# Two input blocks held in SBUF between two sweeps, together with a new table of rank shifts

## The chip, the cores and the metric

The kernel runs on one core of one Trainium2 chip, as one launch. The metric is device microseconds (us) of that core. Most executions agree within 0.3%. The times are about 1.7 us longer than the span of the trace in the same execution.

Five engines matter here: TensorE (PE in the profile, PEld for its weight loads), VectorE (DVE), ScalarE (ACT), GpSimd (POOL) and SyncE (SP). SyncE computes nothing; all loads and stores of any size go through its DMA queue (SPq in the timelines), in the order in which they are issued.

## The reference, cut to what matters

Four residual blocks in a row, linear attention (A), gated unit (B), A again, B again, with shared weights; the outputs are the result and the gradients of x and of all weights. The sequence has 2048 rows of 512, in bfloat16.

```python
x = A_x
x = x + _A_ref(_layernorm(x, axis=-1), A_wqkv, A_wo)
x = x + _B_ref(_layernorm(x, axis=-1), B_w_gate, B_w_up, B_w_down)
x = x + _A_ref(_layernorm(x, axis=-1), A_wqkv, A_wo)
x = x + _B_ref(_layernorm(x, axis=-1), B_w_gate, B_w_up, B_w_down)
...
_out, _vjp = jax.vjp(_f, A_x, A_wqkv, A_wo, B_w_gate, B_w_up, B_w_down)
_grads = _vjp(grad_out)
```

The first A needs its input twice: once for the keys and values of all rows (sweep 1), and again, after the sum over all rows is known, for the residual addition (sweep 2). Between the two lies a barrier.

## The kernel before: the parts that matter

The kernel is a list of pieces. A piece is a short run of instructions with its dependencies, its cost on TensorE and the cost of what follows on other engines. A planner written in Python runs once, while the program is built. It gives each piece a rank (the length of the longest path from it to the end), and plays the pieces through a model of the engines; whenever an engine of the model is free, it gets the ready piece of the highest rank. The order that comes out is fixed into each engine's list of instructions. The table OFFSETS is added to the ranks: a positive shift lets a piece go earlier, a negative one later.

```python
for u in self.pieces:
    u.prio += self.offsets.get(u.key.rpartition(".")[0] if u.key.count(".") > 1 else u.key, 0.0)
```

Sweep 1 loads the eight input blocks (256 rows each) and gives each buffer back after its layer norm. Sweep 2 loads them again, last block first:

```python
def sweep1(k):
    ...
    for b in range(NBLK):
        G.load(f"LX.{b}", lambda b=b: ld(b), BLK, [f"LN0.{b - 3}.1"], "+t2")
        if b == 0:
            G.load("WK", lambda: load_w4(k, wq_[:, D:2 * D], "wk"), 2 * BLK, ["LX.0"], "+w4")
        layernorm(k, 0, b, lambda b=b: xin[b], [[f"LX.{b}", f"LN0.{b - 1}.1@s", f"<GS0.{b - 3}.3"]] * 2)
        G.free("-t2", [f"LN0.{b}.{j}@h" for j in range(2)])
        ...

def sweep2(k):
    ...
    def xin(b):
        t = t2(k, "x0l", [P, 2, D])
        nc.sync.dma_start(out=t[:], in_=tok3(k.x_in, last - b))
        return t
```

The last stage, from about 720 us on, computes the weight gradients: groups of 32 matmuls each. One operand of a group comes from HBM, turned over by a transposing DMA (the tile `dw_set`); a group ends with an evacuation into a small buffer `dw_o` of a ring, and a store:

```python
def load_set(src, r0, n, deps=()):
    nm = f"S{ns[0]}"
    ...
    nc.sync.dma_start_transpose(out=t[:, :, 0:n], in_=src[r0:r0 + n, :])
...
G.store(f"SJ{gi}", lambda: nc.sync.dma_start(out=out_ap, in_=st["o"][0:r, 0:n]), r * n * 2 / 1e6, [f"J{gi}.3"], "-s1")
```

The sets are S0, S1, ...; the groups' matmuls are J0, J1, ... and their stores SJ0, SJ1, ... in the table's language.

Of the kernel before, what the change touches and what calls it, by code (L numbers as in the profile page):

```python
# [25 lines left out]
NBLK = S // TB  # L26
# [48 lines left out]
class Plan:  # L75
# [210 lines left out]
ACCJ, ACCY = 11, 7  # L286
KEEP = (3, 3)
KEEPX, KEEPQ = 3, 2
SBT = {2: range(8), 0: range(0), 1: range(0)}
SUMS = {1: ([0, 1], -1), 3: ([2, 3], 1), 5: ([4, 5], 3), 6: ([6], 5), 7: ([7], 6)}  # L290
MSUMS = {1: ([0, 1], -1), 3: ([2, 3], 1), 5: ([4, 5], 3), 7: ([6, 7], 5)}
PB1 = (0.0, 0.0)
OFFSETS = """
    DE0:3=-81,7=+11 DE2:1=+97 DH2:1=+84 DK0:4=+21 DK2:4=-48 DP0:1=-15,2=+49,3=+71
    DP2:0=-18,2=+21,3=+4,4=+10,5=+30,6=-198 DT0:+67 DW1:1=-50,3=-1 DW3:0=+95,1=+64,4=-2,7=+13 Fg3:11=+28 Fh1:12=-14
    Fh3:4=-25 G1:0=-49,1=-15 G11:7=+97 G3:4=+64,5=+66,7=+38 GS0:2=+20,5=+17,6=-68 GS2:6=+30 K0:0=-18 K2:2=+31
    LB3:4=-3,7=+65 LDH2:6=+11,7=+11 LDL0:5=+36 LDL2:1=-69,2=-7,7=+23 LDP2:6=+2 LDQ2:6=-3 LDX0:4=-5 LG3:0=+58,1=+39
    LN0:2=-53,4=-92,7=-170 LP0:2=-11,3=-11 LQ2:2=-2,3=-15,5=+7 LS1:1=-7 LX:7=+127 LX0:4=+76,5=+35 MS0:5=-306
    MS2:1=-65,3=-1 Q0:1=-63,4=-40,5=-57,7=+64 Q2:2=+18 RX2:2=+69 S1:-43 S30:-17 SG2:-21 SH3:7=-73 SK2:7=-70 SM2:-73
    SN0:2=-193,5=-178,6=-178 SN2:0=-118 SO3:7=-56 SPK2:3=+30 SQ0:1=+127,2=+8 SQ2:7=-122 SU1:5=+8 SV1:1=-89  # L300
    SV3:0=+40,7=-139 TB1:5=-12 TG0:1=+2,2=+6,4=-176,5=-76,6=+6 TG2:4=+100,6=+71 TK0:0=+111,4=+293,5=+613,7=+151
    U0:1=-40 WP2:3=+87 WT2:3=-45 Y1:4=-9 Y33:0=-16,1=-13 YA2:5=+8,6=-1 ZE0:2=+19
    ZE2:0=+69,1=+72,2=+89,3=+160,4=+184,5=+142,6=+105 ZS0:3=+16,5=+30 ZS2:7=+28
"""
BLK = S * D * 2 / 8e6
TOKENS = dict(mm=5, acc=2, tp=1, t2=BUFS["t2"], xb=BUFS["xb"], s1=BUFS["s1"], w4=BUFS["w4"], w11=BUFS["w11"],
# [83 lines left out]
def t2(k, name, shape=None, dt=BF16):  # L390
    return k.p1.tile(shape or [P, NDC, TB], dt, name=name, tag="t2", bufs=BUFS["t2"])
# [420 lines left out]
def a_p2(k, l, b, xin_fn, deps):  # L812

    nc, G = k.nc, k.G
    A = k.A[l]
    st = {}
    n = f"{l}.{b}"
    C = NBLK - 1 - b
    B = b if l else C

    def lx():
        st["xin"] = xin_fn()

    def den():
        pq = A.pq[b]
        ps = tpps(k, [P, 2, H], "den_ps", F32)
        for j in range(2):
            for c in range(NDC):
                nc.tensor.matmul(ps[:, j, :], lhsT=pq[:, c, tslice(j)], rhs=A.Z[:, c, :],
                                 start=(c == 0), stop=(c == NDC - 1))  # L830
        yield
        dn = k.p1.tile([P, 2, H], F32, name="dn", tag="dn", bufs=2)
        nc.vector.tensor_scalar(dn[:], ps[:], EPS, None, ALU.add)
        yield
        r = k.p1.tile([P, 2, H], F32, name="rcp", tag="rcp", bufs=2)
        nc.vector.reciprocal(r[:], dn[:])
        for j in range(2):
            yield
            st["rx", j] = s1(k, "rx")
            src = r[:, j, :].unsqueeze(2).to_broadcast([P, H, D // H])  # L840
            dst = st["rx", j][:].rearrange("p (h e) -> p h e", h=H)
            if l == 0:
                nc.scalar.copy(dst, src)
            else:
                nc.gpsimd.tensor_copy(dst, src)

    def turn(j):
        if j == 0:
            st["rT"] = t2(k, "rTx", [P, 2, NDC, P])
        nc.sync.dma_start_transpose(out=st["rT"][:, j, :, :], in_=st["rx", j][:])  # L850

    def spread(hf):
        if hf == 0:
            A.pn[b] = t2(k, "pnT")
            A.rphi[b] = t2(k, "rphiT")
        sl = slice(2 * hf, 2 * hf + 2)

        def by_tile(t):
            return t[:, sl, :].rearrange("p c (j t) -> p c j t", j=2)
        rT = st["rT"][:, :, sl, :].rearrange("p j c t -> p c j t")  # L860
        nc.vector.tensor_tensor(by_tile(A.pn[b]), by_tile(A.pq[b]), rT, ALU.mult)
        yield
        rphi = by_tile(A.rphi[b])
        nc.vector.tensor_scalar(rphi, by_tile(A.pq[b]), -EPS, 1.0, ALU.add, ALU.min)
        yield
        nc.vector.tensor_tensor(rphi, rphi, rT, ALU.mult)

    def y(j):
        if j == 0:
            k.x[l, b] = xb(k, "xa") if l == 0 else st["xin"]  # L870
        ps = mmps(k, [P, D], "ya_ps")
        for c in range(NDC):
            nc.tensor.matmul(ps[:], lhsT=A.pn[b][:, c, tslice(j)], rhs=A.Wp[:, c, :], start=(c == 0), stop=(c == NDC - 1))  # L873
        yield
        nc.vector.scalar_tensor_tensor(k.x[l, b][:, j, :], ps[:], 1.0, st["xin"][:, j, :], ALU.mult, ALU.add,
                                       accum_out=k.sx[l + 1][:, 2 * b + j:2 * b + j + 1])
    if l and b < KEEPX:
        G.add("LX" + n, lx, 0.0, [f"LN2.{C}.{j}" for j in range(2)])
    else:
        G.load("LX" + n, lx, BLK if l == 0 else 2 * BLK, [f"YA{l}.{b - 2}.1"] + ([f"SX1.{C}"] if l else []) + deps, "+t2" if l == 0 else "+xb")  # L880
    eng = "P" if l else "A"
    G.add("DE" + n, den, 8 * 0.027, [f"Q{n}.0", f"Q{n}.1", f"ZZ{l}", f"<YA{l}.{b - 2}.1"],
          [("V", 0.22, "+dn -tp"), ("V", 0.55, "-dn"), (eng, 0.65, "+s1 @0"), (eng, 0.65, "+s1")], "+tp")
    for j in range(2):
        G.load(f"RX{n}.{j}", lambda j=j: turn(j), BLK, [f"DE{n}" + ("" if j else "@0")] + ([f"~RX{n}.0"] if j else []), "-s1" if j else "+t2 -s1", turn=True)
    for hf in range(2):
        G.add(f"SP{n}.{hf}", lambda hf=hf: spread(hf), 0.0, [f"RX{n}.{j}" for j in range(2)] + ([f"~SP{n}.0"] if hf else []),
              [("V", 0.42, "@pn"), ("V", 0.29), ("V", 0.42)], "" if hf else "+t2 +t2")
    G.free("-t2", [f"SP{n}.{hf}" for hf in range(2)])
    pn = [f"SP{n}.{hf}@pn" for hf in range(2)]  # L890
    G.free("-t2", [f"SP{n}.0", f"SP{n}.1"])
    G.store(f"SN{n}", lambda: nc.sync.dma_start(out=dmaj(k.pnT_d[l], B), in_=A.pn[b][:]), BLK, pn)
    G.store(f"SR{n}", lambda: nc.sync.dma_start(out=k.rphi_d[l][B * P:(B + 1) * P, :], in_=flat(A.rphi[b][:])), BLK, [f"SP{n}.{hf}" for hf in range(2)], "-t2")
    G.free("-t2", [f"SN{n}", f"<YA{n}.1"])
    if l == 0:
        G.free("-t2", [f"YA{n}.{j}" for j in range(2)])
    for j in range(2):
        G.add(f"YA{n}.{j}", lambda j=j: y(j), 4 * C512, pn + ["LX" + n] + [f"WP{l}.{c}" for c in range(NDC)] + ([f"<YA{n}.0"] if j else []),
              [("V", 0.69, "-mm")], "+mm +xb" if j == 0 and l == 0 else "+mm")
# [4 lines left out]
def a_b1(k, l, b, deps):  # L904
# [58 lines left out]
    for j in range(2):  # L963
        G.add(f"CA{n}.{j}", lambda j=j: cast(j), 0.0, [f"LB{lx}.{b}.{j}", "LN_" + n, f"<MS{l}.{b - 2 if b % 2 else b - 3}.3"]
              + ([f"CA{n}.0"] if j else []), [("A", 0.62)], "" if j else "+t2")
    if b in SBT[l]:
        def turn(j):
# [461 lines left out]
def glu_bwd(k, l, b):  # L1429
# [28 lines left out]
    def chunk(p):  # L1458
        w = pw(p)
        cs = slice(2 * p, 2 * p + len(pair_chunks(p)))  # L1460
        dps = (proj_tiles if b in SBT[l] else proj)(k, k.wdT, st["gT"], p, "dhh_ps")
        yield
# [89 lines left out]
def sweep1(k):  # L1552
    nc, G = k.nc, k.G
    k.x, k.dx, k.hT = {}, {}, {}
    xin = {}
    last = NBLK - 1

    def ld(b):
        xin[b] = t2(k, "x0", [P, 2, D])
        nc.sync.dma_start(out=xin[b][:], in_=tok3(k.x_in, b))  # L1560
    wq_ = k.w["wqkv"]
    for b in range(NBLK):
        G.load(f"LX.{b}", lambda b=b: ld(b), BLK, [f"LN0.{b - 3}.1"], "+t2")
        if b == 0:
            G.load("WK", lambda: load_w4(k, wq_[:, D:2 * D], "wk"), 2 * BLK, ["LX.0"], "+w4")
        layernorm(k, 0, b, lambda b=b: xin[b], [[f"LX.{b}", f"LN0.{b - 1}.1@s", f"<GS0.{b - 3}.3"]] * 2)
        G.free("-t2", [f"LN0.{b}.{j}@h" for j in range(2)])
        a_k(k, 0, b, True, b >= TURN0)
        a_q(k, 0, b, True, [] if b < 2 else [f"<K0.{last}.1"])
    G.load("WQ", lambda: load_w4(k, wq_[:, 0:D], "wq"), 2 * BLK, ["LX.2", "WK"], "+w4")  # L1570
    G.load("WV", lambda: load_w4(k, wq_[:, 2 * D:3 * D], "wv"), 2 * BLK, ["LX.4", "WQ"], "+w4")
    G.load("WO", lambda: load_w4(k, k.w["wo"], "wo"), 2 * BLK, ["LX.5", "WV"], "+w4")
    G.free("-w4", ["<K2.%d.1" % last])
    G.free("-w4", [f"<Q2.{last}.1"])
    G.free("-w4", ["<KV2"])
    G.free("-w4", ["<WP2.3"])
    a_barrier(k, 0)


def sweep2(k):  # L1580
    nc, G = k.nc, k.G
    last = NBLK - 1

    def xin(b):
        t = t2(k, "x0l", [P, 2, D])
        nc.sync.dma_start(out=t[:], in_=tok3(k.x_in, last - b))
        return t
# [316 lines left out]
```

## Time and profile before

| | before |
|---|---|
| time, median of the first 3 runs | 1088.78 us (1088.7 to 1089.19) |
| span of the profiled execution | 1084.6 us, mean granted clock 0.998 |
| TensorE busy | 1055.2 us |
| DMA volume | 240.33 MB |
| largest waits of TensorE | 7.0 us start, 2.1 us barrier, 1.8 us first transposed set |

The second row hides something that matters later: 0.998 is not full clock. A stretch of 3.4 us at half clock in a span of 1085 us lowers the mean by 3.4 / 2 / 1085 = 0.0016. So 0.998 is about one such stretch, 0.997 two, 0.995 three, and 1.000 none. The record of the clock begins at about 12 us; the matmuls before it are slow in every kernel (four key matmuls take 1.86 us at 8.79 us and 1.03 us at 221.87 us, before) and are not counted in these means.

### The profile page before, as it was taken

What the parts mean: (1) busy time and instruction counts of PE and PEld (TensorE: products, weight loads), DVE (VectorE), ACT (ScalarE), POOL (GpSimd) and SP (SyncE); (2) the same over time, 40 slices, a digit from 0 to 9 for tenths busy, and PEclk for the clock granted to TensorE, in tenths of its full rate; (3) what the DMA queues carried; (4) which work ended last, traced back from release to release, by engine and by line L of the source; (5) the groups of instructions that cost most, each with busy time, mean ns of one, the idle gap of its engine ahead of it and who ended that gap; (6) DMA issues with size and microseconds to landing.
All of it is one profiled execution on the core that took longest, in us unless ns stands there. A gap on an engine that the chain in (4) does not pass through costs nothing.

```text
span 1084.6 us, 19597 instructions
## 1 busy us (share of the span) xinstructions
PE 1055.2 (97%) x7265; PEld 692.1 (64%) x7360; DVE 637.3 (59%) x1558; ACT 358.0 (33%) x717; POOL 186.7 (17%) x457
## 2 busy tenths in 40 slices
PE   6989999999999999999899999999999999999998
PEld 3667667666566667675566666656554466666787
DVE  6897787689866887788766658768754000000010
ACT  6765565455243333332244433431211000000010
POOL 3145676526012120200000000000000000000000
PEclk9999999999999999999999999999999999999999
DMA  7868898987998777866998799779999999999970
GB/s 237 261 178 277 227 269 246 241 228 194 239 230 210 189 203 192 210 166 162 247 246 257 212 279 285 212 168 237 224 275 267 264 225 216 236 225 227 209 173 20
DMA packets 508208, 240.33 MB, mean 222 GB/s; under 512 B 333808, under 2 KB 493264, under 8 KB 506064
## 3 DMA queue, kind: packets, MB, share of 16 engines
q1 hardware_dynamic: 508112, 239.07, 87.6%
q8 instruction: 57, 0.93, 0.4%
q14 instruction: 39, 0.32, 0.1%
HBM read 61.93 MB, written 95.72 MB: 145 GB/s over the span
## 4 chain that ended last, share of the span: by engine, by line
PE 83%; DVE 5%; DMA 3%; issue 1%; POOL 1%; SPq 1%; ACT 1%; DVEq 0%; ACTq 0%; POOLq 0%
PE dw_ps L1786 25%; PE dha_ps L1155 7%; PE g_ps L1214 6%; PE dh_acc L1296 6%; PE u_ps L1214 6%; PE dhh_ps L1214 6%; PE dh_acc L1294 6%; PE y_acc L1266 3%; PE y_ps L1416 3%; PE dpk_ps L1139 3%; PE m_ps L998 2%; PE ya_ps L873 2%; PE dpn_ps L937 2%; PE k_ps L599 1%; PE g_ps L625 1%
## 5 line engine op out<-in xcount | busy, mean ns | idle before, releaser
L1786 PE MATMUL dw_ps<-dw_set,h 128*128 128x352 bf16 (+2 forms) x1536 | 205.6, 297 | 0.0
L1786 PEld LDWEIGHTS <-h 128*128 128x128 bf16 x1536 | 150.3, 98 | 55.3
L1768 DVE TENSOR_SCALAR dw_o<-dw_ps 128x512 bf16<-128x512 f32 (+3 forms) x33 | 17.6, 541 | 237.8 <-PE dw_ps L1786 218.6
L1296 PE MATMUL dh_acc<-wgT,dg 128*128 128x512 bf16 x346 | 131.1, 379 | 2.3 <-DVE dg L1368 0.6
L1294 PE MATMUL dh_acc<-wuT,du 128*128 128x512 bf16 x324 | 122.8, 379 | 0.3
L1766 ACT ACTIVATE dw_o<-dw_ps 128x512 bf16<-128x512 f32 (+4 forms) x34 | 16.1, 481 | 257.4 <-PE dw_ps L1786 234.0
L1093 POOL TENSOR_SCALAR ab<-c 128x2 f32<-128x2 f32 x64 | 22.2, 348 | 435.1 <-DVE lnb_j L1090 434.7
L1214 PE MATMUL g_ps<-hT,wg 128*128 128x256 bf16 x704 | 92.5, 273 | 0.1
L1214 PE MATMUL u_ps<-hT,wu 128*128 128x256 bf16 x704 | 92.5, 273 | 0.0
L1214 PE MATMUL dhh_ps<-gT,wdT 128*128 128x256 bf16 x704 | 89.0, 273 | 0.7 <-ACT gT L474 0.7
L1214 PEld LDWEIGHTS <-wg 128*128 128x128 bf16 x704 | 68.4, 98 | 21.1
L1786 PE MATMUL dw_ps<-g,dw_set 128*128 128x512 bf16 (+1 forms) x344 | 77.0, 379 | 2.6 <-DMA dw_set<-hh_d 1.8
L1214 PEld LDWEIGHTS <-wdT 128*128 128x128 bf16 x704 | 68.5, 98 | 13.2 <-issue 0.8
L1214 PEld LDWEIGHTS <-wu 128*128 128x128 bf16 x704 | 68.9, 98 | 8.0
L1786 PEld LDWEIGHTS <-dw_set 128*128 128x128 bf16 (+1 forms) x352 | 35.1, 100 | 41.1 <-DMA dw_set<-hh_d 2.1
L1296 PEld LDWEIGHTS <-dg 128*128 128x128 bf16 x352 | 34.4, 98 | 36.1 <-DVE dg L1368 1.2
L1294 PEld LDWEIGHTS <-du 128*128 128x128 bf16 x352 | 34.4, 98 | 34.9 <-DVE du L1469 0.3
L1087 ACT ACTIVATE lnb_t<-dha_ps,rstd 128x512 f32<-128x512 f32 x32 | 22.0, 687 | 85.0 <-PE dha_ps L1155 45.9
L1349 ACT ACTIVATE th<-g_ps 128x512 f32<-128x512 f32 (+1 forms) x48 | 26.6, 558 | 65.4 <-PE g_ps L1214 53.0
L1469 DVE TENSOR_TENSOR du<-s2tl,dhh 128x512 bf16<-128x512 bf16 (+1 forms) x48 | 19.0, 402 | 46.4 <-ACT dhh L1464 41.0
L1255 DVE SCALAR_TENSOR_TENSOR hh<-th,u_ps 128x512 bf16<-128x512 f32 (+1 forms) x48 | 30.5, 640 | 21.3 <-ACT th L1250 13.3
L1266 PE MATMUL y_acc<-wd,hh 128*128 128x512 bf16 x168 | 40.7, 379 | 0.6 <-DVE hh L1255 0.2
(188 smaller groups left out, 1794.1 us busy)
## 6 DMA issues: line engine op xcount, KB each, us to landing
s2t_d<-s2t SPq DMA_DIRECT2D x8, 1408.0 KB, 6.4
s2tl<-s2t_d SPq DMA_DIRECT2D x8, 1408.0 KB, 8.2
hh_d<-hh SPq DMA_DIRECT2D x16, 640.0 KB, 4.7
du_d<-du SPq DMA_DIRECT2D x80, 128.0 KB, 2.7
dg_d<-dg SPq DMA_DIRECT2D x80, 128.0 KB, 2.9
h_d<-h SPq DMA_DIRECT2D x32, 256.0 KB, 2.6
h<-h_d SPq DMA_DIRECT2D x18, 256.0 KB, 4.6
pk_d<-pk SPq DMA_DIRECT2D x16, 256.0 KB, 3.8
```

Source lines behind the costliest of these rows:

```text
L1087: nc.scalar.activation(t[:], dh_ps, ACT.Identity, scale=rs, accum_out=c12[:, 0:1])
L1093: nc.gpsimd.tensor_scalar(ab[:], c12[:], -1.0 / D, 0.0, ALU.mult, ALU.add)
L1139: nc.tensor.matmul(ps[:, c2, :], lhsT=A.U[:, m, cslice(2 * hf + c2)], rhs=st["hT"][:, m, :], start=(m == 0), stop=(m == NDC - 1))
L1155: nc.tensor.matmul(ps[:], lhsT=lh[:, c, tslice(j)], rhs=rh[:, c, :], start=(i + c == 0), stop=(i == 2 and c == NDC - 1))
L1214: nc.tensor.matmul(ps[:, i, :], lhsT=w[:, m, fsl(fc)], rhs=rhsT[:, m, :], start=(m == 0), stop=(m == NDC - 1))
L1255: nc.vector.scalar_tensor_tensor(hh, th[:, 0:w], 1.0, flat(up[:])[:, 0:w], ALU.add, ALU.mult)
L1266: nc.tensor.matmul(st["acc"][j][:], lhsT=st["hh"][:, fc, tslice(j)], rhs=k.wd[:, fc, :], start=(fc == 0), stop=(fc == NFC - 1))
L1294: nc.tensor.matmul(acc[j][:], lhsT=du[:, i, tslice(j)], rhs=k.wuT[:, fc, :], start=(fc == 0), stop=False)
L1296: nc.tensor.matmul(acc[j][:], lhsT=dg[:, i, tslice(j)], rhs=k.wgT[:, fc, :], start=False, stop=(fc == NFC - 1))
L1349: nc.scalar.activation(th[:, 0:w], flat(gp[:])[:, 0:w], ACT.Tanh, scale=0.5)
L1416: nc.tensor.matmul(ps[:], lhsT=st["hh"][:, fc, tslice(j)], rhs=k.wd[:, fc, :], start=(fc == 0), stop=(fc == NFC - 1))
L1786: nc.tensor.matmul(ps, lhsT=lhs(s_), rhs=rhs(s_), start=(s_ == 0), stop=(s_ == 31))
```

## The change

The last two blocks of sweep 1 keep their buffers, and sweep 2, which begins with the last block, takes them from SBUF. That saves two loads of 0.262 MB. The table OFFSETS is new throughout. The core of the diff:

```diff
+KEEP0 = 2
 OFFSETS = """
-    DE0:3=-81,7=+11 DE2:1=+97 DH2:1=+84 DK0:4=+21 DK2:4=-48 DP0:1=-15,2=+49,3=+71
+    CB1:1=-105,2=-98 CG0:0=-85 DE0:0=-47,3=-85,5=+6,6=+6 DE2:0=-2 DH2:0=-144 DP0:1=-13,5=+1
     ... (all ten lines of the table are new)
-    if l and b < KEEPX:
-        G.add("LX" + n, lx, 0.0, [f"LN2.{C}.{j}" for j in range(2)])
+    if b < (KEEPX if l else KEEP0):
+        G.add("LX" + n, lx, 0.0, [f"LN{l}.{C}.{j}" for j in range(2)])
...
-    xin = {}
+    xin = k.xin = {}
...
-        G.free("-t2", [f"LN0.{b}.{j}@h" for j in range(2)])
+        if b < NBLK - KEEP0:
+            G.free("-t2", [f"LN0.{b}.{j}@h" for j in range(2)])
...
     def xin(b):
+        if b < KEEP0:
+            return k.xin[last - b]
         t = t2(k, "x0l", [P, 2, D])
```

More of the change, by code (lines that the diff above doesn't have):

```diff
@@ L293 @@
 OFFSETS = """
-    DE0:3=-81,7=+11 DE2:1=+97 DH2:1=+84 DK0:4=+21 DK2:4=-48 DP0:1=-15,2=+49,3=+71
-    DP2:0=-18,2=+21,3=+4,4=+10,5=+30,6=-198 DT0:+67 DW1:1=-50,3=-1 DW3:0=+95,1=+64,4=-2,7=+13 Fg3:11=+28 Fh1:12=-14
-    Fh3:4=-25 G1:0=-49,1=-15 G11:7=+97 G3:4=+64,5=+66,7=+38 GS0:2=+20,5=+17,6=-68 GS2:6=+30 K0:0=-18 K2:2=+31
-    LB3:4=-3,7=+65 LDH2:6=+11,7=+11 LDL0:5=+36 LDL2:1=-69,2=-7,7=+23 LDP2:6=+2 LDQ2:6=-3 LDX0:4=-5 LG3:0=+58,1=+39
-    LN0:2=-53,4=-92,7=-170 LP0:2=-11,3=-11 LQ2:2=-2,3=-15,5=+7 LS1:1=-7 LX:7=+127 LX0:4=+76,5=+35 MS0:5=-306
-    MS2:1=-65,3=-1 Q0:1=-63,4=-40,5=-57,7=+64 Q2:2=+18 RX2:2=+69 S1:-43 S30:-17 SG2:-21 SH3:7=-73 SK2:7=-70 SM2:-73
-    SN0:2=-193,5=-178,6=-178 SN2:0=-118 SO3:7=-56 SPK2:3=+30 SQ0:1=+127,2=+8 SQ2:7=-122 SU1:5=+8 SV1:1=-89
-    SV3:0=+40,7=-139 TB1:5=-12 TG0:1=+2,2=+6,4=-176,5=-76,6=+6 TG2:4=+100,6=+71 TK0:0=+111,4=+293,5=+613,7=+151
-    U0:1=-40 WP2:3=+87 WT2:3=-45 Y1:4=-9 Y33:0=-16,1=-13 YA2:5=+8,6=-1 ZE0:2=+19
-    ZE2:0=+69,1=+72,2=+89,3=+160,4=+184,5=+142,6=+105 ZS0:3=+16,5=+30 ZS2:7=+28
+    CB1:1=-105,2=-98 CG0:0=-85 DE0:0=-47,3=-85,5=+6,6=+6 DE2:0=-2 DH2:0=-144 DP0:1=-13,5=+1
+    DP2:0=-18,2=+9,3=-4,4=+10,5=+30,7=-39 DT2:-123 DW1:1=-50,2=-2,3=-1,6=-26 DW3:0=+85,1=+64,4=-9 E3:1=-11
+    Fg3:11=+28 Fh1:8=-24 Fh3:10=-6 G1:0=-152 G11:5=-9,6=-11,7=+130 G3:0=+55,2=-1 GS0:1=-14,6=-58 GS2:6=+58 J12:2=+73
+    K0:4=-33,7=-25 K2:2=+31 LB2:2=-17 LB3:6=-3 LDH2:0=+188 LDL2:0=+139,1=-94 LG3:0=+89,1=+49 LH1:7=-67
+    LN0:0=-71,1=-208,4=-78,5=-126,6=-93 LN2:0=-11,1=-11,2=-20,7=-94 LN3:2=-63 LN_0:6=+98 LP2:6=-70 LX:2=-16,5=+9
+    LX0:4=+97,5=+40 MS0:5=-372 MS2:3=+19,5=-2 Q0:1=-50,2=-23,4=-98,6=-26 Q2:3=-23,7=+71 RX0:0=+94,2=+142,5=+23
+    RX2:6=+9 S1:-21 SH0:1=-26,7=+84 SH1:4=+13 SHH3:7=+80 SM2:+126 SP2:2=-48,3=+137,4=+40,7=+49 SPK2:0=+10 SQ0:2=+9
+    SQ2:7=-28 SU1:0=-25,4=+13,5=+21,6=-29 SU3:7=-69 SV3:0=+70 SX1:2=+68 TB1:0=-52,5=-10
+    TG0:1=+2,2=+6,4=-265,5=-87,6=+6 TK0:1=+82,2=+576,4=-6,5=+421,6=+95 TR3:0=-15 U2:2=-133 WDZ:-50 WGT0:+68 Y1:4=-9
+    Y33:0=-20,1=-17,4=-35 YA2:7=+56 ZB0:+35 ZE0:0=-31,1=-21 ZE2:0=+84,1=+122,3=+107,4=+200,5=+177 ZN0:+73
 """
```

## The prediction

> **What bounds the kernel now.** I read the page first, then the table by stages, then the waits of TensorE, then the timeline of the one bad stretch, then the tile that the change removes.
>
> The page gives the ceiling. The first line is the span; the PE line has TensorE's busy time and share; the traffic line has what the DMA queues moved (the page adds that 61.93 MB of it were read from HBM).
>
> ```profile
> span 1084.6 us, 19597 instructions
> ...
> PE 1055.2 (97%) x7265; PEld 692.1 (64%) x7360; DVE 637.3 (59%) x1558; ACT 358.0 (33%) x717; POOL 186.7 (17%) x457
> ...
> DMA packets 508208, 240.33 MB, mean 222 GB/s; under 512 B 333808, under 2 KB 493264, under 8 KB 506064
> ```
>
> TensorE is idle for 1084.6 - 1055.2 = 29.4 us in all. The change takes no matmul away, so apart from stretches at a low clock, 29.4 us is all that it can win. Two per cent of 1088.8 us is 21.8 us.
>
> The table by stages (columns: PE, PEld, DVE, ACT, POOL busy, granted clock, DMA share, GB/s) says where the 29.4 us are:
>
> ```profile
> 0.00:25.00 25.00, 16.22 (x103) 8.41 (x106) 15.39 (x45) 16.74 (x27) 9.99 (x37) 1.00 0.77 239
> 25.00:50.00 25.00, 24.09 (x210) 15.33 (x212) 19.84 (x56) 18.64 (x33) 4.80 (x12) 1.00 0.92 294
> 50.00:75.00 25.00, 21.87 (x186) 15.88 (x187) 23.16 (x63) 17.95 (x36) 8.39 (x26) 0.93 0.61 159
> 75.00:100.00 25.00, 24.60 (x185) 17.46 (x187) 18.88 (x41) 11.71 (x24) 15.33 (x32) 1.00 0.76 220
> ```
>
> Idle: 8.8 us in the first 25 us, 0.9 in the next, 3.1 around the barrier between the sweeps (50 to 75 us), 0.4 after it. So the two sweeps that the change touches hold 13.2 us of the idle time in their first 100 us. The rest of the run, whose stages I read the same way, has 3.1 us at 200 to 300, 3.6 at 500 to 600, 3.1 at 700 to 800, 3.4 at the end, and under 1 elsewhere.
>
> The waits of TensorE by name (total, times, longest), cut to the largest:
>
> ```profile
> PE hTk_ps L472 <- ACT h L561: 7.0, 1, 7.0
> PE hT_ps L472 <- ACT h L537: 3.0, 2, 2.1
> PE hTk_ps L472 <- ACT hTk L474: 2.1, 3, 0.7
> PE dw_ps L1786 <- DMA dw_set<-hh_d: 1.8, 1, 1.8
> ```
>
> The reader is to see that none waits for the tile x0l, the reload that the change removes. The 7.0 us are the start-up: the first layer norm needs x, then DVE, GpSimd and ACT, before TensorE has a thing to transpose. The 2.1 us are the barrier. In the timeline of TensorE there:
>
> ```profile
> 61.70 1.91 PE L797 MATMUL q_ps<-hTk,wq 128*128 128x256 bf16 x16
> 65.74 0.40 PE L472 MATMUL hT_ps<-ident,h 128*128 128x128 bf16 x4 [2.13 <-ACT h L537]
> 65.97 3.08 PE L873 MATMUL ya_ps<-Wp,pnT 128*128 128x512 bf16 x8
> 68.85 0.63 PE L472 MATMUL hT_ps<-ident,h 128*128 128x128 bf16 x4
> 70.15 0.35 PE L829 MATMUL den_ps<-Z,pqT 128*128 128x32 bf16 x8 [0.67 <-ACT hT L474]
> ```
>
> The query matmuls are used up, TensorE stands for 2.13 us until the first layer norm of sweep 2 is through, and then eight matmuls take 68.85 - 65.97 = 2.88 us.
>
> **What the Trainium skill says.** "TensorE: Matmul & The Clock Gate", section "Wait — 56ns, not 53.3ns?", gives one 512-column matmul per 215.7 ns with a warm clock, twice that cold. The trace agrees: eight should take 8 x 0.2157 = 1.73 us (an estimate from that page), they took 2.88, so the short gap cost another 1.15 us; the granted clock in the window from 65 to 70 us is 0.66. The page puts the change to cold at about 3.4 us of idleness; here 2.13 us were enough. "Perfetto Trace Analysis", section "Identifying the Most-Contended Engine", warns that matmul busy time is no measure of the roofline; so I use the busy share only to find gaps, as its section "Optimization Strategy" tells: find the gaps on the engine that matters and what ends each. "SBUF — State Buffer", section "SBUF: two separate sides", says that DMA and engine ports cannot contend; the evacuations that read x0l took 677 to 693 ns in all sixteen cases, under every DMA load, which fits. So fewer loads will not make the engines' instructions shorter.
>
> **The change part by part.**
>
> 1. Two loads fall away. The tile's own view:
>
> ```profile
> L1586 SPq DMA_DIRECT2D x0l<-in_A_x_dram x8: 464/508/1320, 2.3 to 170.9; - x8
> ...
> DMA to landing us min/median/max: 3.0/3.7/6.5
> ```
>
> The eight loads become six. Each moves 256 x 512 x 2 bytes = 0.262 MB, so 0.524 MB of 240.33 go (0.2%), some 2.4 us of the queue at its mean 222 GB/s, and 2 x 0.5 us of issue. When were the two issued? In the timeline of the DMA queue:
>
> ```profile
> 0.79 1.49 SPq L1560 DMA_DIRECT2D x<-in_A_x_dram  x3
> 2.32 0.47 SPq L1586 DMA_DIRECT2D x0l<-in_A_x_dram  x1
> 2.83 0.47 SPq L1510 DMA_DIRECT2D wk<-in_A_wqkv_dram  x1
> 3.34 0.51 SPq L1586 DMA_DIRECT2D x0l<-in_A_x_dram  x1
> ```
>
> At 2.32 and 3.34 us, nearly 60 us before the first use at 60.84 us. They were fillers, and the x that the first norm needs is ahead of them. The only neighbour they can hold up is wk, issued at 2.83, which lands 5.9 us later, at 8.73, while the first key matmul starts at 8.79. That looks like a wait, but it isn't worth what it looks: the four cold transposes just ahead of it on TensorE start at 8.30 and need 4 x 0.107 = 0.43 us (cold pace, estimate from the page named above), so TensorE was free only at 8.73. wk may come 0.5 to 1 us earlier; **gain 0 to 0.3 us**.
>
> 2. Two buffers of the ring of 21 are held otherwise. Before: two x0l from 2 us to about 61 and 69 us. After: the last two x tiles, loaded at about 21 and 24 us, until the same uses. So there are two buffers more from 2 to about 22 us, and as many as before later. No wait of TensorE in that time is for a buffer of this ring: the waits at 8.30, 21.76 and 34.80 us (0.67, 0.70, 0.73) are for ACT's copy out of the one transpose bank. **Gain 0 to 0.5 us.**
>
> 3. The table of rank shifts is new throughout. It costs no instruction. It changes the order in which each engine's fixed list is laid down, in all five sweeps and the weight gradients, so it alone can move the 29.4 us. What it could reach: the interior waits of 0.2 us and more, taken from the timeline of TensorE, add up to 14.4 us (the first 7.02 left out), plus 1.15 us of low clock. Start and end (7.0 and 2.9 us, the last matmul ends at 1081.65) stay. So about **15.5 us are the whole prize**, 1.4%. Nobody gets all: the waits for the transpose bank are built in. The barrier is the best target: 2.13 + 1.15 + 0.67 = 3.95 us. There ACT ran an exponential (64.39 to 64.99) ahead of the norm's last step, though GpSimd's figure was ready at 64.07; ACT's order alone cost 0.8 us, and one query group of 1.75 us kept for the gap would fill most of it. I assume that the table was searched anew for the new list, and that it wins back part of the barrier (about 2 us) and 1 to 2 us among the waits at 252, 540 and 724 us (1.54, 1.85, 2.58 us).
>
> Sum: 0.15 + 0.2 + about 3 = 3.4 us. 1088.8 - 3.4 is **about 1085.4 us**.
>
> **The rivals.**
>
> A. The loads are hidden and the table is only as good as the old one. For it: no wait names x0l, and each table seems the outcome of a long search, with diminishing returns. Time 1087 to 1089.5.
>
> B. The table is worse on the chip than on whatever model ranked it: a rank shift puts a DMA-fed piece first in an in-order list and TensorE stands, as at 729.66 us now (1.80 us for a transposed load of 7.9 us). Then new gaps of 1 to 3 us each, with cold matmuls behind them. Against it: somebody kept it. Time 1090 to 1095.
>
> C. The barrier is closed completely and some later gaps too. For it: the change leaves a tidier queue just before the barrier. Against it: DVE is busy 5.00 of 5.00 us from 55 to 60 and from 60 to 65, so the chain there is nearly limited by DVE as well. Time 1079 to 1083.
>
> **Range and chances.** My own theory has about half of the weight, A about 30%, B and C about 10% each. That gives 1085.4 us with a range of 1080.5 to 1089.5. Faster by over 2% needs 1067 us, which is beyond the 15.5 us that can be won: 0.01. Slower by over 2% needs 21.8 us of new gaps: 0.01. Within 2%: 0.98.
>
> **What would show each step.** DMA volume near 239.8 MB and HBM reads near 61.4 MB; six x0l loads, none before 60 us; wk issued near 2.3 us; but the first key matmul still at 8.4 to 8.9 us (step 1). No new wait named x in the first 60 us, and TensorE's idle time from 10 to 50 us within 0.7 us of now (step 2). TensorE idle 24.5 to 27.5 us instead of 29.4; in 50 to 75 us over 22.5 us busy and a clock above 0.93 (step 3). PE instructions unchanged, apart from records that are missing. I am wrong if the first 25 us lose over 1 us, for then the two early loads did hold up the start; or if TensorE's idle time falls by over 8 us or grows, for then the table did more than I allow.

## The result, and the profile after

| | before | after |
|---|---|---|
| median of 6 runs of the same rounds | 1088.78 us (1086.25 to 1089.33) | 1088.25 us (1084.62 to 1089.97) |
| ratio after : before | | 0.9995, 95% interval 0.9976 to 1.0014: same |
| span of the profiled execution | 1084.6 us | 1086.2 us |

A ratio in this document is the mean time of one kernel's runs over that of the other's of the same rounds, so it is not quite the ratio of the medians that are quoted. The two profiled executions lie the other way round from the medians, by 1.6 us; both are within the spread of their kernels. What follows explains those two executions, and then asks which of the differences come back in others.

From the page of the kernel after:

```profile
span 1086.2 us, 19658 instructions
...
PE 1061.9 (98%) x7360; PEld 692.6 (64%) x7360; DVE 637.6 (59%) x1558; ACT 358.1 (33%) x717; POOL 185.9 (17%) x457
...
DMA packets 507664, 239.80 MB, mean 221 GB/s; under 512 B 333776, under 2 KB 492720, under 8 KB 505520
```

The volume fell by 0.53 MB, as it must. But read the PE line with care: 7360 matmuls and 7360 weight loads. The page of the kernel before had 7265 and 7360. Ninety-five matmul records are missing there, and the gaps that they leave counted as idle time. So "97%" and "98%" cannot be compared, and the 29.4 us of idleness from which the prediction starts were too many: keep_old_table below, with the same table and all records, has 1084.2 - 1060.5 = 23.7 us, and the kernel after 1086.2 - 1061.9 = 24.3. Added up from the timelines, the waits of 0.2 us and more are about 21.4 us before and 21.0 us after.

The table by stages of the kernel after (PE, PEld, DVE, ACT, POOL busy, granted clock, DMA share, GB/s), for the start and the barrier:

```profile
0.00:25.00 25.00, 16.32 (x87) 8.17 (x88) 15.11 (x45) 16.93 (x27) 9.93 (x37) 1.00 0.72 230
...
50.00:75.00 25.00, 22.32 (x210) 16.81 (x208) 24.38 (x67) 18.82 (x37) 9.05 (x25) 1.00 0.65 168
```

The clock at the barrier is now 1.00 instead of 0.93. TensorE's timeline there, in the kernel after:

```profile
65.73 0.40 PE L473 MATMUL hT_ps<-ident,h 128*128 128x128 bf16 x4 [0.93 <-DVE zk L758]
66.11 1.90 PE L874 MATMUL ya_ps<-Wp,pnT 128*128 128x512 bf16 x8
...
69.64 0.35 PE L830 MATMUL den_ps<-Z,pqT 128*128 128x32 bf16 x8 [1.16 <-ACT hT L475]
```

The wait before the first transposes is 0.93 us instead of 2.13, the same eight matmuls take 1.90 us instead of 3.08, and the wait before `den_ps` has grown from 0.67 to 1.16. A small wait ahead of these lines has grown by 0.2 us. So the barrier gave back 1.2 + 1.15 - 0.5 - 0.2, about 1.7 us, where the prediction assumed about 2. Then the waits of TensorE by name (total, times, longest), in the kernel after:

```profile
PE dw_ps L1790 <- DMA dw_set<-hh_d: 2.9, 1, 2.9
...
PE dw_ps L1790 <- ACT dw_o L1770: 1.8, 1, 1.8
```

The first has grown from 1.8 us, the second is new. Both belong to the weight gradients, 650 us after the code that was changed. Where the two kernels meet that stage is best seen in four lines of TensorE's timeline. Before:

```profile
716.95 0.60 PE L1214 MATMUL dhh_ps<-gT,wdT 128*128 128x256 bf16 x4
...
729.66 1.90 PE L1786 MATMUL dw_ps<-g,dw_set 128*128 128x512 bf16 x8 [1.80 <-DMA dw_set<-hh_d]
...
734.01 3.62 PE L998 MATMUL m_ps<-pn,g 128*128 128x512 bf16 x16
...
865.85 7.07 PE L1786 MATMUL dw_ps<-g,dw_set 128*96 128x512 bf16 x32 [0.38 <-DMA out_dram<-dw_o]
```

And after:

```profile
714.36 0.60 PE L1215 MATMUL dhh_ps<-gT,wdT 128*128 128x256 bf16 x4
...
728.20 2.66 PE L1790 MATMUL dw_ps<-g,dw_set 128*128 128x512 bf16 x8 [2.93 <-DMA dw_set<-hh_d]
...
734.22 3.62 PE L999 MATMUL m_ps<-pn,g 128*128 128x512 bf16 x16
...
867.44 7.07 PE L1790 MATMUL dw_ps<-g,dw_set 128*96 128x512 bf16 x32 [1.76 <-ACT dw_o L1770]
```

The start times, compared line by line, are the ledger:

| where | after is ahead by | what happened since the line above |
|---|---|---|
| first key matmul (8.79 before, 8.62 after) | 0.2 us | `wk` is issued 0.5 us earlier |
| last `dhh_ps` of the last sweep | 2.6 us | above all the barrier, and waits between 200 and 300 us that are gone |
| first weight-gradient group | 1.5 us | wait for the first set: 2.93 instead of 1.80 us |
| `m_ps` | -0.2 us | the same matmuls cold: 734.22 - 728.20 = 6.0 instead of 4.35 us |
| eleventh group | -1.6 us | wait for a `dw_o` buffer: 1.76 instead of 0.38 us |
| end | -1.6 us | nothing |

TensorE won 2.6 us and gave back 4.2. The second row is not fully explained: up to there the waits of 0.2 us and more add up to 18.4 us before and 15.6 after, which with the 1.15 us of clock at the barrier would give a lead of 4.0. The other 1.4 us are not accounted for here. The clock behind the fourth row is in the table by stages of the kernel after, for 725 to 735 us; the last three columns are granted clock, DMA share, GB/s:

```profile
725.00:730.00 5.00, 2.07 (x10) 0.81 (x8) 2.79 (x15) 0.00 (x0) 0.00 (x0) 0.92 1.14 244
730.00:735.00 5.00, 5.00 (x27) 2.69 (x25) 2.32 (x8) 1.69 (x3) 0.00 (x0) 0.74 1.04 214
```

The shortfall is (0.08 + 0.26) x 5 us / 0.5 = 3.4 us at half clock. In the kernel before both stretches show 1.00. So the half-clock stretch was not removed: it left the barrier and turned up at 729 us.

Why did the first wait grow? In the timeline of the DMA queue, the kernel before and then the kernel after:

```profile
721.73 4.97 SPq L1754 DMA_TRANSPOSE dw_set<-hh_d  x1
```

```profile
719.61 5.66 SPq L1758 DMA_TRANSPOSE dw_set<-hh_d  x1
```

TensorE came 2.6 us earlier, the load 2.1 us, and it needed 8.5 us to land instead of 7.9. The set waits in the queue behind two other transposed loads and two stores, and the whole chain moves only in part with TensorE.

### The profile page after: what moved, and what is told of

The parts are those of the page before. It is cut to its first block, busy times and chain, and to the rows that moved or that the text cites. A ratio compares the mean times of both kernels' runs of the same rounds, so it can differ in the third digit from the quotient of the medians.

```text
span 1086.2 us, 19658 instructions
## 1 busy us (share of the span) xinstructions
PE 1061.9 (98%) x7360; PEld 692.6 (64%) x7360; DVE 637.6 (59%) x1558; ACT 358.1 (33%) x717; POOL 185.9 (17%) x457
## 2 busy tenths in 40 slices
DMA packets 507664, 239.80 MB, mean 221 GB/s; under 512 B 333776, under 2 KB 492720, under 8 KB 505520
## 3 DMA queue, kind: packets, MB, share of 16 engines
HBM read 61.41 MB, written 95.72 MB: 145 GB/s over the span
## 4 chain that ended last, share of the span: by engine, by line
PE 90%; DMA 1%; DVE 1%; SPq 1%; ACT 1%; issue 0%; POOL 0%; DVEq 0%; ACTq 0%
PE dw_ps L1790 25%; PE dha_ps L1156 7%; PE g_ps L1215 7%; PE u_ps L1215 7%; PE dhh_ps L1215 7%; PE dh_acc L1297 7%; PE dh_acc L1295 7%; PE y_acc L1267 3%; PE y_ps L1417 3%; PE m_ps L999 2%; PE ya_ps L874 2%; PE dpn_ps L938 2%; PE dpk_ps L1140 2%; PE q_ps L798 1%; PE g_ps L626 1%; PE k_ps L600 1%
## 5 line engine op out<-in xcount | busy, mean ns | idle before, releaser
L1297 PE MATMUL dh_acc<-wgT,dg 128*128 128x512 bf16 x352 | 133.4, 379 | 0.0
L1295 PE MATMUL dh_acc<-wuT,du 128*128 128x512 bf16 x352 | 133.4, 379 | 0.0
L1267 PE MATMUL y_acc<-wd,hh 128*128 128x512 bf16 x176 | 42.9, 379 | 0.0
```

The lines of the kernel that those rows point to most:

```text
L1267: nc.tensor.matmul(st["acc"][j][:], lhsT=st["hh"][:, fc, tslice(j)], rhs=k.wd[:, fc, :], start=(fc == 0), stop=(fc == NFC - 1))
L1295: nc.tensor.matmul(acc[j][:], lhsT=du[:, i, tslice(j)], rhs=k.wuT[:, fc, :], start=(fc == 0), stop=False)
L1297: nc.tensor.matmul(acc[j][:], lhsT=dg[:, i, tslice(j)], rhs=k.wgT[:, fc, :], start=False, stop=(fc == NFC - 1))
```

## The experiments

Twelve kernels ran in three jobs, each on another chip, all correct. Each was timed in 5 rounds beside the kernel before, whose median was 1085.22 us in job 1, 1088.96 in job 2 and 1090.57 in job 3 (11 runs each). Compare within a job; the ratios are against the kernel before of the same job.

| job | kernel | median (range), us | ratio, 95% interval |
|---|---|---|---|
| 1 | keep_old_table | 1085.65 (1084.57 to 1091.26) | 1.0004, 0.9983 to 1.0026 |
| 1 | reload_new_table | 1086.02 (1084.23 to 1086.92) | 0.9994, 0.9976 to 1.0011 |
| 1 | reload_no_table | 1125.34 (1124.61 to 1127.58) | 1.0364, 1.0343 to 1.0384 |
| 1 | keep_no_table | 1127.89 (1123.06 to 1130.27) | 1.038, 1.0356 to 1.0404 |
| 2 | dead2 | 1089.55 (1087.44 to 1091.68) | 1.0002, 0.9982 to 1.0022 |
| 2 | after_warm | 1086.88 (1084.18 to 1091.27) | 0.9985, 0.9962 to 1.0009 |
| 2 | after_s0first | 1088.27 (1086.51 to 1089.02) | 0.9993, 0.9975 to 1.0012 |
| 2 | before_s0first | 1091.5 (1090.76 to 1092.7) | 1.0027, 1.0009 to 1.0045 |
| 3 | after_again | 1088.85 (1086.08 to 1093.71) | 0.9986, 0.9962 to 1.001 |
| 3 | after_stores | 1107.72 (1105.11 to 1108.63) | 1.0147, 1.0123 to 1.0172 |
| 3 | after_stores_warm | 1105.13 (1104.73 to 1109.14) | 1.0137, 1.0114 to 1.0161 |
| 3 | before_stores | 1106.2 (1105.77 to 1109.34) | 1.0147, 1.0124 to 1.0169 |

### Job 1: the two parts, each alone and with no table

The question is whether one part gains and the other loses. Theory 1 held that the loads are hidden and that each table fits its own list only, so that an exchanged table is no better (ratio 0.999 to 1.010 for keep_old_table, 1.000 to 1.010 for reload_new_table). Theories 2 and 3 held that one part gains or costs 2 us or more and that the other takes it back.

**keep_old_table**, the kernel after with the table of before:

```diff
 OFFSETS = """
-    CB1:1=-105,2=-98 CG0:0=-85 DE0:0=-47,3=-85,5=+6,6=+6 ...
+    DE0:3=-81,7=+11 DE2:1=+97 DH2:1=+84 DK0:4=+21 ...   (all of the table of before)
```

> Keeps the two input blocks in SBUF as the change does, with the table of rank shifts of the kernel before. Theory 1 (the loads were hidden, and any table is worth what its gaps are worth): the keys of the old table were tuned for another list, so it should be no better than either kernel, ratio to the kernel before 0.999 to 1.010; no new wait of TensorE names x or x0l. Theory 2 (keeping helps by 2 to 4 us, and the new table takes it back): ratio 0.996 to 0.998. Theory 3 (keeping costs, because two buffers of the ring are tied up, and the new table makes it good): ratio 1.002 or more with a new wait in the first 70 us.

Measured: 1.0004. Its profile has the barrier of the kernel before (2.1 us of wait, half clock behind it), a first set that is waited for 1.85 us, and no wait at the eleventh group. So these marks of the kernel before come with the old table, not with the reloads.

**reload_new_table**, the kernel before with the table of after:

```diff
 OFFSETS = """
-    DE0:3=-81,7=+11 DE2:1=+97 DH2:1=+84 DK0:4=+21 ...
+    CB1:1=-105,2=-98 CG0:0=-85 DE0:0=-47,3=-85,5=+6,6=+6 ...   (all of the table of after)
```

> The kernel before with only the table exchanged: all eight reloads are made. Theory 1: the table fits its own list only, ratio to the kernel before 1.000 to 1.010, gaps in other places. Theory 2 (the table, not the keeping, carries the loss): ratio 1.002 or more with the same long wait for the first transposed load of the weight gradients (2.9 us). Theory 3: the table alone wins 2 to 4 us, ratio 0.996 to 0.998.

Measured: 0.9994. The barrier is that of the kernel after, 0.9 us before the transposes and a full clock. The wait at the eleventh group is there (4.0 us), with a half-clock stretch behind it. The wait for the first set is only 0.8 us. There is a wait of 0.7 us for `wk` at the start, which no other kernel of this job has. Its queue there is that of the kernel before, to the same hundredth of a microsecond (`x0l` at 2.32, `wk` at 2.83, `x0l` at 3.34 us), yet the first key matmul comes at 9.42 us instead of 8.79:

```profile
9.42 1.01 PE L599 MATMUL k_ps<-wk,hTk 128*128 128x512 bf16 x2 [0.68 <-DMA wk<-in_A_wqkv_dram]
```

**reload_no_table** and **keep_no_table**, both kernels with an empty table:

```diff
 OFFSETS = """
-    ...
 """
```

> The kernel before with an empty table. Base line of the pair that follows. All theories: slower than the kernel before, since the table is what the search produced: ratio 1.005 to 1.03.

> The changed kernel with an empty table: the structural part of the change without any tuning. Theory 1: within 0.3% of the run with an empty table and the reloads (difference under 3 us either way, the sign is chance). Theory 2: 2 to 4 us faster than it. Theory 3: 2 us or more slower than it.

Measured: 1125.34 and 1127.89 us, some 40 us or 3.7% above the kernels with a table, with mean clocks of 0.988 to 0.992. What follows: a table is worth 3.7%, either table serves either kernel, and keeping the blocks gains nothing by itself that these runs can resolve, which is about 2 us (with no table it stands 2.5 us higher in the median and 1.8 in the mean, with overlapping intervals; 2.5 us lies in the bands of theories 1 and 3 alike). So the first half of theory 1 stands; that a table fits its own list only does not. The fourth corner of the square, the kernel after itself, was timed in the first result and in job 3, not in this job.

### dead2: were the two early loads free by nature?

The two loads were hidden in the kernel before. But only one of them stood ahead of `wk` there, so that alone does not show that loads are free at that place. This kernel is the kernel after, with two loads of the same 0.262 MB put into the queue ahead of `wk`, into a buffer that is overwritten later:

```diff
+            def wk():
+                k.wg_tile = w11(k, [P, NDC, F], "wg")
+                for i in range(DEAD):
+                    nc.sync.dma_start(out=k.wg_tile[...], in_=tok3(k.x_in, last - i))
+                load_w4(k, wq_[:, D:2 * D], "wk")
+            G.load("WK", wk, 2 * BLK, ["LX.0"], "+w4")
```

> The changed kernel, order of every engine untouched, but with two dead loads of the same two input blocks (0.262 MB each) put back on the DMA queue just ahead of wk, into a buffer that is overwritten later. It measures the removed loads by themselves. Theory 1 (hidden): wk is issued about 1 us later and lands 1 to 2 us later, the first key matmul starts 0 to 0.5 us later, and the time is within 0.5 us of the changed kernel, ratio to the kernel before 0.999 to 1.001. Rival (the early loads held up the start): first key matmul 1 us or more later and the time 1 us or more longer than the changed kernel's.

In its trace `wk` is issued at 3.33 us, and TensorE's timeline shows the start:

```profile
9.54 1.86 PE L601 MATMUL k_ps<-wk,hTk 128*128 128x512 bf16 x4 [0.89 <-DMA wk<-in_A_wqkv_dram]
```

The first key matmul starts 0.92 us later than in the kernel after (8.62). So the expected 0 to 0.5 us were too little: two loads ahead of `wk` cost about 0.9 us in this execution. The number of loads ahead does not settle it, however. Five profiled executions have the queue of the kernel before at the start, with one load ahead of `wk` (before, before_s0first, before_stores, reload_no_table, reload_new_table). From the second transposes to the first key matmul they took 0.49, 0.69, 0.67, 0.38 and 1.27 us, against 0.37 or 0.38 in the other kernels with the blocks kept; dead2 took 1.48. So one load ahead of `wk` cost between 0 and 0.9 us. What makes the difference is not shown. The whole time does not show it (1.0002). A look at the rest of the trace shows why such an amount gets lost: the wait at the eleventh group was 5.5 us in this execution, and two half-clock stretches in a row followed, with the same order of instructions there as in the kernel after.

### after_warm: is the half-clock stretch behind the wait a cost?

Ten matmuls without use fill the wait for the first set; the group's first real matmul overwrites what they leave:

```diff
+            if gi == 0 and i == 0:
+                for _ in range(WARM):
+                    nc.tensor.matmul(ps, lhsT=k.ident[:], rhs=rhs(0), start=True, stop=True)
             for s_ in range(8 * i, 8 * i + 8):
```

> The changed kernel with ten extra matmuls of 512 columns (results overwritten) on TensorE just ahead of the first weight-gradient matmul, where TensorE waits 2.93 us for a transposed load; they take some 2.2 us of the gap. Theory: the gap drops TensorE to half clock for one window of 3.4 us, which costs about 1.7 us behind it; with the gap filled the clock stays at 1.0 from 725 to 740 us and the time falls by about 1.5 us, ratio to the kernel before about 0.998. Rival (the low clock there is chance or costs nothing): no change, ratio 0.9995.

The trace shows the first group behind them at full clock, eight matmuls in 1.89 us instead of 2.66:

```profile
727.91 1.89 PE L1794 MATMUL dw_ps<-g,dw_set 128*128 128x512 bf16 x8
```

The stretch at 729 us is gone, and by the next `m_ps` (732.25 us) this execution is 2 us ahead of the kernel after. But it had a half-clock stretch between 538.9 and 542.3 us, which the kernel after had not. The ratio, 0.9985, has the expected direction and an interval that includes 1. Three of its six runs had a mean clock of 1.000, against 2 of 12 of the unaltered kernel after; those three took 1084.18, 1085.14 and 1085.64 us. So the clock term is real, in the trace; whether the fill is a gain in the mean is not settled.

### after_s0first and before_s0first: move the first transposed load ahead

If the first set arrives late because it is queued late, a shift of its rank should put it ahead of the transposed loads and stores in front of it:

```diff
-    ... ZE2:0=+84,1=+122,3=+107,4=+200,5=+177 ZN0:+73
+    ... ZE2:0=+84,1=+122,3=+107,4=+200,5=+177 ZN0:+73 S0:+300
```

(and the same item at the end of the table of before).

> The changed kernel with one rank shift more: the first transposed load of the weight gradients goes on the DMA queue ahead of two other transposed loads and two small stores, about 4.5 us earlier. Theory 1 (what the new table won in the first 300 us is lost because TensorE waits 2.9 us for this load, and then runs cold): the wait at 725 to 728 us falls under 0.5 us, the clock stays at 1.0 there, and the time falls by 3 to 5 us: 1083 to 1085.5, ratio to the kernel before 0.995 to 0.997. Rival (the load cannot start earlier because its buffer comes free late, or the two delayed loads become the wait): unchanged, ratio 0.999 to 1.001.

> The same rank shift on the kernel before, whose wait for that load is 1.80 us without a low clock behind it. Theory 1: the time falls by 1 to 2 us, ratio 0.998 to 0.999, so less than for the changed kernel. Rival: unchanged.

The load was issued at 715.56 us, 4.05 us earlier. TensorE's timeline of after_s0first:

```profile
722.89 1.90 PE L1790 MATMUL dw_ps<-g,dw_set 128*128 128x512 bf16 x8 [1.55 <-DMA dw_set<-hh_d]
...
733.12 3.55 PE L1790 MATMUL dw_ps<-g,dw_set 128*128 128x512 bf16 x8 [2.25 <-DMA dw_set<-hh_d]
```

The wait went from the first set to the second: 1.55 + 2.25 = 3.8 us instead of 2.93, and the third quarter of the first group runs cold. The expected 3 to 5 us of gain did not come (0.9993), and before_s0first is slower by 0.27%, with waits of 2.22 and 2.08 us in its profile. But this is no clean test of the load's place in the queue, because the shift also moved the work that uses it. The planner now puts the first eight matmuls of the group ahead of the 32 `dpn_ps` matmuls of 3.65 us, behind which they stand in the kernel after, so that TensorE asks for the set at 721.34 us instead of 725.27. The second set, too, is issued earlier (725.29 us instead of 728.85) and asked for earlier still. What is shown is that this rank shift does not help; whether an earlier load alone would, with TensorE's order kept, was not tested. (The wait at the eleventh group did not come in the profile of after_s0first.)

### after_again: do the two late waits come back?

The kernel after, unaltered, on a third chip.

> The changed kernel unaltered, as the control for the two runs that follow on the same chip. All theories: ratio to the kernel before 0.998 to 1.001, and in its trace the wait ahead of the twelfth weight-gradient group (near 867 us) is anywhere from 1.5 to 5.5 us, as it was in runs whose order there is the same.

It was 0.9986, and so again the same. In its profiled execution the wait for the first set was 2.3 us and that at the eleventh group 2.9 us, both followed by a half-clock stretch. (The recorded texts call it the twelfth group; 320 matmuls, ten groups of 32, run before it, so it is J10, the eleventh.) With the new table, the wait at the eleventh group has been 1.76, 2.9, 2.9 and 5.5 us in four profiles of one and the same order (after, after_again, after_warm, dead2). It is a weak point of the new table, of a size that differs from one execution to the next.

The profiles of the nine kernels without moved stores and with a table, taken together, show the same exchange. The three with the old table (before, keep_old_table, before_s0first) have a half-clock stretch at the barrier: their granted clock from 60 to 80 us is 0.91. None of the six with the new table has one there, and each of the six has one or two elsewhere: from 720 to 740 us (after, after_again, after_s0first), from 860 to 880 us (after_again, dead2, reload_new_table), or near 540 us (after_warm). So in these profiles the table moves the stretch rather than removing it. It is not always at the barrier with the old table: before_stores, below, has the same wait of 2.13 us there and no half clock behind it, and one of the 11 runs of the kernel before in job 1 had a mean clock of 1.000.

### after_stores, after_stores_warm and before_stores: let the stores go first

At the eleventh group an evacuation waits for a `dw_o` buffer, whose store is queued behind transposed loads. So I moved the stores of the first twelve groups ahead:

```diff
+    SJ0:+400 SJ1:+400 SJ2:+400 SJ3:+400 SJ4:+400 SJ5:+400 SJ6:+400 SJ7:+400 SJ8:+400 SJ9:+400 SJ10:+400 SJ11:+400
 """
```

> The changed kernel with the stores of the first twelve weight-gradient groups moved forward on the DMA queue by rank shifts (they now stand behind transposed loads of 5 to 8 us each, so that the seven buffers of the evacuations fill up and TensorE waits near 867 us for a PSUM bank). Theory 1 (the new table gives back here, and by the load of the first transposed set at 728 us, what it wins in the first 300 us): the wait near 867 us goes to 0, the time falls by 2 to 4 us against the unaltered changed kernel of this job, ratio to the kernel before 0.996 to 0.998. Rival (these stores only move the wait: the transposed loads come later by as much): a new wait of TensorE for a transposed load after 740 us, and no change in time.

> The same with the ten extra matmuls in the gap ahead of the first weight-gradient matmul. Theory 1 with the clock: another 0.5 to 1.7 us less, no window of half clock in its trace after 700 us, ratio to the kernel before 0.995 to 0.9975: the fastest kernel of the study. Rival: as without the extra matmuls.

> The same shifts of the stores on the kernel before, whose wait near 866 us is 0.38 us. Theory 1: 0 to 1.5 us faster, ratio 0.9985 to 1.000. Rival (the shifts help by something else than that wait): as large a gain as for the changed kernel.

All three are misses: their medians are 15 to 17 us above that of the kernel before. The wait at the eleventh group is gone, and another has come. TensorE's timeline of after_stores, and the line of its DMA queue that released it:

```profile
893.97 11.29 PE L1791 MATMUL dw_ps<-dw_set,h 128*128 128x352 bf16 x65 [15.17 <-DMA h<-h_d]
```

```profile
890.67 0.57 SPq L1739 DMA_DIRECT2D h<-h_d  x1
```

A plain load of `h`, issued at 865.40 us in the kernel after, now goes at 890.67, behind three transposed loads that hold the queue for 5.8 to 7.7 us each. One wrong place in this queue costs 15 us, over eight times the 1.76 us that the move took away. The DMA share is 1.13 (before) and 1.16 (after) from 860 to 880 us, which suggests that there is little slack in the queue there.

## Why the prediction was right, point by point

The prediction was "same", 1085.4 us within 1080.5 to 1089.5. The result, 1088.25 us, is the same and inside the range, but it is rival A (1087 to 1089.5), and not the theory that had half of the weight. Of the 3.4 us forecast, 0.5 came; the number was met by the width of the range and not by the sum.

**Step 1, the two loads: right for these two executions, too general in its reason.** The volume is 239.80 MB, HBM reads are 61.41 MB, six `x0l` loads remain with the first at 71.1 us, `wk` goes at 2.32 us, the first key matmul at 8.62 us, in the announced 8.4 to 8.9. The gain of 0.17 us (0.11 if counted from the first transpose) lies in 0 to 0.3. The prediction took the loads to be free because only the four transposes stood between; the five executions with that queue show a cost of 0 to 0.9 us, and reload_new_table alone lies outside 0 to 0.3. With both loads ahead of `wk` (dead2) it was 1.1 by the same measure.

**Step 2, the two buffers: right.** No new wait names x in the first 60 us. TensorE is idle for 1.80 us from 10 to 50 us instead of 2.00, within the announced 0.7. No gain can be seen.

**Step 3, the table: right in the direction and the place, mis-sized in the sum.** The prediction said: "I assume that the table was searched anew for the new list, and that it wins back part of the barrier (about 2 us) and 1 to 2 us among the waits at 252, 540 and 724 us". Up to 715 us that is roughly what happened: 2.6 us of lead. The barrier gave 1.7; the waits from 200 to 300 us fell from 2.45 us to none of 0.2 us or more, and 0.8 us at 302 and 0.6 us at 528 were new. The step that failed is the silent one: that a lead of TensorE is kept to the end. The term for the wait at the first set ("724 us") was booked as a gain of a part of 1.80 us and measured as a loss of 1.13 us; the half-clock stretch behind it, 1.67 us, and the longer wait at the eleventh group, 1.38 us, were not in the sum at all. Then 2.6 - 1.1 - 1.7 - 1.4 = -1.6 us, as the ledger has it. Job 1 says the same without any trace: the two tables differ by less than the runs do.

**Rival B was partly at work.** It named the place (729.66 us, a transposed load of 7.9 us) and the kind, "new gaps of 1 to 3 us each, with cold matmuls behind them". It gave the net loss too high, since it left out what the table wins before.

**The announced signs.** Clock above 0.93 from 50 to 75 us: 1.00, right. TensorE busy over 22.5 us there: 22.32, missed narrowly, and weakened by records that were missing before. The idle time of 24.5 to 27.5 us can't be judged: it came to 24.3 us, but was to be read against 29.4, which counted the gaps of 95 missing records as idleness. The waits by name, 21.4 and 21.0 us, show a gain of 0.4 us where step 3 had about 3.

**What stays open.** Whether the kernel after is faster by about 0.1%: its ratios of 0.9995 and 0.9986 both have intervals that include 1. Whether after_warm's 0.15% is real. What sets the size of the wait at the eleventh group in a given execution. And no run changed the table in one stage alone, so which of its items made the barrier better was not tested. The ledger is that of one pair of executions. No kernel clearly beats both.

## What to carry to other kernels

A load that no wait names is worth its place in the queue and nothing more; look at what stands behind it, then leave it. Before a gain early in a program is booked, find the next place where the engine waits for something that doesn't move with it (here a queue of transposed loads), because a lead arrives there as a longer wait, and can come out cold. Whether it does depends on how the gap lies in the windows of the clock (see below), so do not read a cold stretch in one profile as a property of the kernel. And count the matmul records against the weight loads before an idle share is used as a budget.

## What the Trainium skill lacked or had wrong

- "TensorE: Matmul & The Clock Gate", section "What's actually happening", gives the cold state after at least one idle window of about 3.4 us, and says that the window runs freely. Here it came behind shorter gaps: 2.13 us (barrier, before), 2.25 us (after_s0first), 2.93 us (after). It didn't come behind gaps of 1.80 us (before), 2.22 and 2.08 us (before_s0first). And 2.9 us at the eleventh group were followed by a cold group in after_again, 32 matmuls in 8.75 us, and by a warm one in after_warm, 32 in 7.07 us. So between 2.1 and 2.9 us it can go either way. The clock events kept with the traces (`trace.npz`; no view of `prof` prints them) say which way. From the first event, at 11 to 13 us, the clock changes only at whole multiples of 3.413 us in all 14 profiled executions, so the page is right that a window runs freely, and its length agrees. But a window need not be idle from end to end. Of the 28 windows at full clock in which TensorE was busy for under 46% of the time, 27 were followed by half clock (the exception, 42% busy, is at the barrier of before_stores); of the 4355 that were busy for over 47%, none was. The gap of after_again lay in one window, busy for 25%; that of after_warm lay across two, busy for 48% and 67%. The two groups, in TensorE's timeline of after_again and then of after_warm:

```profile
867.14 8.75 PE L1790 MATMUL dw_ps<-g,dw_set 128*96 128x512 bf16 x32 [2.94 <-ACT dw_o L1770]
```

```profile
867.73 7.07 PE L1794 MATMUL dw_ps<-g,dw_set 128*96 128x512 bf16 x32 [2.86 <-ACT dw_o L1771]
```

- "DMA: Bandwidth & Descriptors", section "Latency and other measured facts", gives 261 GB/s for a transposing DMA with a non-contiguous middle dimension. For a load of this size no page says how long one holds its issuing queue: the first set, 256 x 2048 x 2 bytes = 1.05 MB, held it for 4.97 us (before) and 5.66 us (after) and landed 7.9 and 8.5 us after its issue, which is 133 and 123 GB/s from issue to landing. What stood behind it in the queue was issued only then (725.31 us, after).
- "Perfetto Trace Analysis" does not say that a trace can lack matmul records, whose gaps then read as idle time: 7265 of 7360 were there in the profile of the kernel before, and 94 to 96 were missing in nine of the 14 profiles here.
